# A four-batch cross-covariance attention kernel with a mixture of adapters: loads, gating and output in pieces of 10 token columns, and the passes of neighbouring batches interleaved

## The chip, the cores and the metric

The kernel runs on one core of one Trainium2 chip. The metric is device time in microseconds (us) of that core. Every kernel was run several times; a run counts as fast or slow by its state, and every ratio and every profile below is of fast runs alone. A profile has its span, from the first to the last instruction (309.3 us before). The span after is 1.8 us shorter than the device time of the same execution (296.5), so spans are compared with spans and device times with device times.

## The reference, cut to what matters

```python
# q, k, v: (B, N, C) = (4, 6400, 256) float32; tau = 1
qn = q / (norm(q, axis=1) + 1e-6)          # norms over the 6400 tokens, per channel
kn = k / (norm(k, axis=1) + 1e-6)
s  = kn.transpose(0, 2, 1) @ qn / tau      # (B, 256, 256)
a  = softmax(s, axis=-1)
x  = v @ a                                 # (B, 6400, 256), then seen as (25600, 256)
# mixture of adapters: 8 experts of rank 16, the best two of each token
logits = x @ w_gate                        # (25600, 8)
w      = softmax over the two largest logits
out    = x + sum over the two experts e of w_e * (x @ A[e]) @ B[e]
```

Within a batch everything waits for `a`, and `a` needs all of q and k of the batch. The softmax is a serial step between two passes over the tokens. Batches do not depend on each other.

## The kernel before

The 6,400 tokens of a batch lie on 128 partitions, so a batch is 50 *token columns* of 128 tokens. The loads convert float32 to bf16. For each batch there is a Gram pass over q and k (products k·q, k·k and q·q, all summed in one accumulator `acc`), a softmax chain on the 256 x 256 result, a pass that transposes v and computes the logits of all 50 columns, the gating of all 50 columns at once, and a pass that computes y and the adapters' part, two columns (a *chunk*) at a time.

```python
CPC = 2            # columns of a chunk
LPC = 16           # columns of a load: pieces of 16, 16, 16 and 2
qk_pool: bufs=4, v_pool: bufs=4, vt_pool: bufs=1, y_pool: bufs=2, gwork: bufs=1
psum_acc: bufs=1   # one accumulator for all batches

def emit_loads(b):                      # all q,k pieces, then all v pieces
    for (ps, plen) in load_pieces:
        nc.gpsimd.dma_start(qt[:, :plen, :], q_v[b, :, ps:ps + plen, :])
        nc.gpsimd.dma_start(kt[:, :plen, :], k_v[b, :, ps:ps + plen, :])
    for (ps, plen) in load_pieces:
        nc.gpsimd.dma_start(vt[:, :plen, :], v_v[b, :, ps:ps + plen, :])

def emit_G_init(b, st):                 # clears acc by a matmul with zeros
    for ic in range(CC):
        nc.tensor.matmul(acc[:, ic, :], zeros_bf[:1, :P], zeros_bf[:1, :],
                         start=True, stop=False, skip_group_check=True)
# ... emit_G_piece: 6 matmuls per column into acc (256, 128 and 128 columns, twice)
# ... emit_chain_part1..4: norms (nq_bc), s_sb, a_exp, a_bf; emit_naw: aT, waA
# ... emit_transpose_logits_group: vT_batch and logB, four columns at a time

def emit_ycopy(b, st, ch):
    y_stage, off, gi = get_y_stage(b, st, ch)     # a buffer of 16 columns, of 2
    nc.scalar.copy(y_stage[:, off * CPC:(off + 1) * CPC, :], y_ps)
    # after the last chunk of a group (8 chunks): one DMA out of up to 2 MB

for b in range(B):
    # softmax chain of b, with the last 4 chunks of batch b-1 between its parts
    # transposes and logits of all 50 columns, then the gating
    gpos = {2: 0, 7: 1, 13: 2, 17: 3}   # Gram pieces of b+1 after these chunks
    for c2 in range(main_end):
        emit_passC_chunk_tail(b, st, c2)
        if c2 + npro < main_end:
            emit_zyf(b, st, c2 + npro)
        if b + 1 < B and c2 in gpos:
            emit_G_piece(b + 1, states[b + 1], gpos[c2])
```

So the kernel before already puts Gram work of the next batch between the chunks of this batch, but in four lumps, and its transposes run alone.

Of the kernel before, what the change touches and what calls it, by code (L numbers as in the profile page):

```python
# [10 lines left out]
FP32 = mybir.dt.float32  # L11
# [7 lines left out]
def kernel(  # L19
# [20 lines left out]
    assert ER == P and C % P == 0 and N % P == 0  # L40

    if not isinstance(tau, float):
        tau = float(tau)
    inv_tau = 1.0 / tau

    CPC = 2
    LPC = 16
    NCH = NC // CPC
    KD = min(4, max(0, NCH - 2))

# [5 lines left out]
    def pieces(step, total):  # L56
        res = []
        s = 0
        while s < total:
            res.append((s, min(step, total - s)))  # L60
            s += step
        return res

    load_pieces = pieces(LPC, NC)

    def y_groups_of(b):
        last = (b + 1 == B)
        tail_start = NCH - (min(2, KD) if last else KD)
        groups = []
        s = 0  # L70
        while s < tail_start:
            e = min(s + 8, tail_start)
            groups.append((s, e - s))
            s = e
        if tail_start < NCH:
            groups.append((tail_start, NCH - tail_start))
        return groups

    const = ctx.enter_context(tc.tile_pool(name="const", bufs=1))
    qk_pool = ctx.enter_context(tc.tile_pool(name="qk", bufs=4))  # L80
    v_pool = ctx.enter_context(tc.tile_pool(name="vp", bufs=4))
    vt_pool = ctx.enter_context(tc.tile_pool(name="vtb", bufs=1))
    y_pool = ctx.enter_context(tc.tile_pool(name="yp", bufs=2))
    bat = ctx.enter_context(tc.tile_pool(name="bat", bufs=2))
    gwork = ctx.enter_context(tc.tile_pool(name="gwork", bufs=1))
    work = ctx.enter_context(tc.tile_pool(name="work", bufs=3))
    psum_acc = ctx.enter_context(tc.tile_pool(name="psacc", bufs=1, space=bass.MemoryType.PSUM))
    psum_logB = ctx.enter_context(tc.tile_pool(name="pslog", bufs=1, space=bass.MemoryType.PSUM))
# [3 lines left out]
    ident = const.tile([P, P], BF16)  # L92
    make_identity(nc, ident)

    ones_bf = const.tile([P, P], BF16)
    nc.vector.memset(ones_bf, 1.0)

    zeros_bf = const.tile([P, 512], BF16)
    nc.vector.memset(zeros_bf, 0.0)

    neg_inv_tau = const.tile([P, 1], FP32)
    nc.vector.memset(neg_inv_tau, -inv_tau)

    wg_sb = const.tile([P, CC, E], BF16)
    nc.gpsimd.dma_start(wg_sb, moe_w_gate.rearrange("(cc p) e -> p cc e", p=P))

    A_sb = const.tile([P, CC, E, R], BF16)
    moe_A_v = moe_A.rearrange("e (cc p) r -> p cc e r", p=P)
    for cc in range(CC):
        nc.gpsimd.dma_start(A_sb[:, cc, :, :], moe_A_v[:, cc, :, :])  # L110
    A_sb = A_sb.rearrange("p cc e r -> p cc (e r)")

    ball_sb = const.tile([P, C], BF16)
    nc.gpsimd.dma_start(ball_sb, moe_B.rearrange("e r d -> (e r) d"))

    def emit_loads(b):
        st = {}
        q_tiles, k_tiles, v_tiles = {}, {}, {}
        for (ps, plen) in load_pieces:
            qt = qk_pool.tile([P, LPC, C], BF16, tag="q_piece", name="qt")  # L120
            nc.gpsimd.dma_start(qt[:, :plen, :], q_v[b, :, ps:ps + plen, :])
            kt = qk_pool.tile([P, LPC, C], BF16, tag="k_piece", name="kt")
            nc.gpsimd.dma_start(kt[:, :plen, :], k_v[b, :, ps:ps + plen, :])
            q_tiles[ps] = qt
            k_tiles[ps] = kt
        for (ps, plen) in load_pieces:
            vt = v_pool.tile([P, LPC, C], BF16, tag="v_piece", name="vt")
            nc.gpsimd.dma_start(vt[:, :plen, :], v_v[b, :, ps:ps + plen, :])
            v_tiles[ps] = vt
        st["q_tiles"] = q_tiles  # L130
        st["k_tiles"] = k_tiles
        st["v_tiles"] = v_tiles
        return st

    def emit_G_init(b, st):
        acc = psum_acc.tile([P, CC, 512], FP32, tag="acc", name="acc")
        st["acc"] = acc
        for ic in range(CC):
            nc.tensor.matmul(  # L139
                acc[:, ic, :], zeros_bf[:1, :P], zeros_bf[:1, :],  # L140
                start=True, stop=False, skip_group_check=True)

    def emit_G_piece(b, st, pi):
        acc = st["acc"]
        ps, plen = load_pieces[pi]
        qt, kt = st["q_tiles"][ps], st["k_tiles"][ps]
        for lc in range(plen):
            c = ps + lc
            last = (c == NC - 1)
            for ic in range(CC):  # L150
                nc.tensor.matmul(  # L151
                    acc[:, ic, 0:256],
                    kt[:, lc, ic * P:(ic + 1) * P],
                    qt[:, lc, :],
                    start=False, stop=False, skip_group_check=True)
            for ic in range(CC):
                nc.tensor.matmul(  # L157
                    acc[:, ic, 256:384],
                    kt[:, lc, ic * P:(ic + 1) * P],
                    kt[:, lc, ic * P:(ic + 1) * P],  # L160
                    start=False, stop=False, skip_group_check=True)
            for ic in range(CC):
                nc.tensor.matmul(  # L163
                    acc[:, ic, 384:512],
                    qt[:, lc, ic * P:(ic + 1) * P],
                    qt[:, lc, ic * P:(ic + 1) * P],
                    start=False, stop=last, skip_group_check=True)

    def emit_G(b, st):
        emit_G_init(b, st)  # L170
        for pi in range(len(load_pieces)):
            emit_G_piece(b, st, pi)

    def emit_chain_part1(b, st):
        acc = st["acc"]
        nk2 = bat.tile([P, CC], FP32, name="nk2")
        kscr = bat.tile([P, CC, P], BF16, name="kscr")
        qqI = bat.tile([P, CC, P], BF16, name="qqI")
        for ic in range(CC):
            nc.vector.scalar_tensor_tensor(  # L180
                out=qqI[:, ic, :], in0=acc[:, ic, 384:512], scalar=1.0,
                in1=ident, op0=OP.mult, op1=OP.mult)
# [5 lines left out]
        st["nk2"] = nk2  # L188
        st["qqI"] = qqI

    def emit_chain_part2(b, st):
        nq2_bc = psum_A.tile([P, 256], FP32, tag="psA", name="nq2_bc")
        nc.tensor.matmul(nq2_bc, ones_bf,
                         st["qqI"].rearrange("p c d -> p (c d)"),
                         start=True, stop=True)
        lnk = bat.tile([P, CC], FP32, name="lnk")
        nc.scalar.activation(lnk, st["nk2"], ACT.Ln)
        rk = bat.tile([P, CC], FP32, name="rk")
        nc.scalar.activation(rk, lnk, ACT.Exp, scale=-0.5)
        lnq = bat.tile([P, 256], FP32, name="lnq")  # L200
        nc.scalar.activation(lnq, nq2_bc, ACT.Ln)
        rq_bc = bat.tile([P, 256], FP32, name="rq_bc")
        nc.scalar.activation(rq_bc, lnq, ACT.Exp, scale=-0.5)
        st["rk"] = rk
        st["rq_bc"] = rq_bc

    def emit_chain_part3(b, st):
        acc = st["acc"]
        rk, rq_bc = st["rk"], st["rq_bc"]
        s_sb = bat.tile([P, CC, 256], FP32, name="s_sb")  # L210
        for ic in range(CC):
            nc.vector.scalar_tensor_tensor(
                out=s_sb[:, ic, :], in0=acc[:, ic, 0:256],
                scalar=rk[:, ic:ic + 1], in1=rq_bc,
                op0=OP.mult, op1=OP.mult)
        a_exp = bat.tile([P, CC, 256], BF16, name="a_exp")
        sumexp = bat.tile([P, CC], FP32, name="sumexp")
        for ic in range(CC):
            nc.scalar.activation(a_exp[:, ic, :], s_sb[:, ic, :], ACT.Exp,
                                 bias=neg_inv_tau[:, 0:1], scale=inv_tau,  # L220
                                 accum_out=sumexp[:, ic:ic + 1])
        st["a_exp"] = a_exp
        st["sumexp"] = sumexp

    def emit_chain_part4(b, st):
        recip = bat.tile([P, CC], FP32, name="recip")
        nc.vector.reciprocal(recip, st["sumexp"])
        a_bf = bat.tile([P, CC, 256], BF16, name="a_bf")
        for ic in range(CC):
            nc.vector.tensor_scalar(out=a_bf[:, ic, :],  # L230
                                    in0=st["a_exp"][:, ic, :],
                                    scalar1=recip[:, ic:ic + 1], scalar2=None,
                                    op0=OP.mult)
        st["recip"] = recip
        st["a_bf"] = a_bf

    def emit_naw(b, st):
        a_exp, recip = st["a_exp"], st["recip"]
        aT_ps = psum_A.tile([P, CC, 256], BF16, tag="psA", name="aT_ps")
        n_tr = CC * CC  # L240
# [339 lines left out]
```

## Time and profile before

The median of the runs beside the changed kernel is 311.87 us (310.38 to 312.39, four runs).

The first lines of the page of the kernel before: busy time, then 40 slices of 7.7 us with the busy tenths of TensorE (PE), its granted clock in tenths and the share of the 16 DMA engines in use, then the two main DMA queues (packets, MB, share of the 16 engines' span).

```profile
span 309.3 us, 7431 instructions
PE 256.8 (83%) x3264; PEld 220.9 (71%) x3264; DVE 118.2 (38%) x377; ACT 103.9 (34%) x198; POOL 29.2 (9%) x58
...
PE   1079595999999966999999966999999978979981
...
PEclk9999997699999998999999995799999999999997
DMA  7999999999999999999999999999850055202467
...
q0 software_dynamic: 9408, 39.46, 63.2%
q1 hardware_dynamic: 2304, 26.22, 20.3%
```

The row of TensorE has a dip at 31 to 54 us (the first softmax chain), then two that are two slices wide (66, at 108 to 124 and 178 to 193 us) and a shallow one near 250 us: these are the boundaries between batches. The row of the DMA is full (nines) until about 217 us, has an eight until 224 us, and is thin afterwards. TensorE and the DMA therefore both matter, at different times.

The waits of TensorE and of ScalarE in the kernel before; columns: engine, line, what was waited for, then us in total, times, the longest.

```profile
PE acc L151 <- DMA kt<-in_k_dram: 18.4, 2, 14.8
PE y_ps L392 <- ACT y_stage L440: 14.6, 11, 2.9
PE acc L139 <- DVE s_sb L212: 3.3, 1, 3.3
...
ACT y_stage L440 <- PE y_ps L430: 116.7, 60, 8.4
ACT y_stage L440 <- DMA out_dram<-y_stage: 6.4, 2, 3.3
```

The copy of y waits twice, 3.3 us at most, until an output DMA has emptied a buffer. First ScalarE, then TensorE around 190 us; columns: start, us, engine, line, operation, and in brackets the idle time before it and its releaser.

```profile
189.72 1.07 ACT L440 COPY y_stage<-y_ps 128x512 f32<-128x512 f32 x2 [3.26 <-DMA out_dram<-y_stage]
190.68 0.52 ACT L219 ACTIVATE a_exp<-s_sb,neg_inv_tau 128x256 bf16<-128x256 f32 x1
```

The windows view by batch; columns: window, its length, busy time of TensorE, weight loads, VectorE, ScalarE and GpSimd with instruction counts, granted clock, DMA share (1 reads as all 16 engines in use; it can be slightly above), GB/s.

```profile
51.00:121.00 70.00, 63.11 (x805) 55.35 (x805) 29.17 (x86) 24.39 (x47) 7.39 (x14) 0.94 1.03 246
121.00:190.00 69.00, 62.95 (x816) 54.13 (x814) 29.47 (x88) 25.24 (x49) 6.34 (x12) 0.95 1.03 262
190.00:260.00 70.00, 65.10 (x834) 56.33 (x834) 30.71 (x94) 27.14 (x53) 2.11 (x4) 0.95 0.67 193
260.00:309.00 49.00, 38.44 (x511) 31.84 (x509) 26.67 (x100) 22.61 (x43) 0.00 (x0) 0.97 0.38 157
```

Busy time of TensorE overstates its work, because matmuls overlap (by the page, a key-query matmul of 256 columns lasts 277 ns in the mean, and the next one can start after 109). I therefore took the start times of successive matmuls from the trace and split the time from the first norm matmul (the start of the first softmax chain) to the last matmul into four parts:

- *issue*: what the matmuls need when nothing is in the way, with the usual intervals of the trace (109 ns for 256 columns, 55.5 for 128, 25 for 8). For the zero matmuls of 512 columns, 216 ns is an estimate: 109 plus twice the 53.5 that the step from 128 to 256 columns adds (in the trace of the kernel before, the next matmul follows them after 400 ns or more, five of the eight times at half clock).
- *long gaps*: the excess over the usual interval of the full clock, for the single intervals where it is 1 us or more, whatever the clock was.
- *half clock*: all other excess in stretches in which the granted clock was half.
- *small stalls*: the rest.

| us | first norm matmul | issue | long gaps | half clock | small stalls | last matmul starts | span |
|---|---|---|---|---|---|---|---|
| before | 46.9 | 201.2 | 17.9 | 9.7 | 27.3 | 302.9 | 309.3 |

The first norm matmuls of the four batches start at 46.9, 110.5, 179.9 and 250.7 us.

### The profile page before, as it was taken

Reading aid. Unit: us, or ns where it says so; the run is one execution under the profiler, and the core shown is the slowest. Engines: PE = TensorE matmul, PEld = TensorE weight load, DVE = VectorE, ACT = ScalarE, POOL = GpSimd, SP = SyncE. Lnnn points to the kernel's source line nnn. Section 1 sums busy time; section 2 is a strip of 40 time slices with the busy share of each in tenths; the row PEclk is TensorE's granted clock in tenths of the full one; section 3 lists DMA queues with packets and bytes.
Section 4 is the critical chain, followed back from the end, with each engine's and each line's share of the span. In section 5 each row is a group of like instructions: output and inputs, shape, how many; then the busy total and the mean of one; then the engine's idle time right before and its main releaser. Section 6 shows DMA issues by size and latency. Waiting matters only on the chain.

```text
span 309.3 us, 7431 instructions
## 1 busy us (share of the span) xinstructions
PE 256.8 (83%) x3264; PEld 220.9 (71%) x3264; DVE 118.2 (38%) x377; ACT 103.9 (34%) x198; POOL 29.2 (9%) x58
## 2 busy tenths in 40 slices
PE   1079595999999966999999966999999978979981
PEld 0069493997898854897888854997898856867770
DVE  0000004475312344475312344466412246794540
ACT  1000005432322272642322272542313266744451
POOL 8210120201110110110010110020000000000000
PEclk9999997699999998999999995799999999999997
DMA  7999999999999999999999999999850055202467
GB/s 48 214 212 220 212 213 217 215 212 219 214 307 251 215 309 298 281 256 212 217 318 246 215 316 301 269 257 214 190 245 2 32 242 219 90 2 104 172 271 305
DMA packets 11744, 66.14 MB, mean 214 GB/s; under 512 B 3392, under 2 KB 5056, under 8 KB 5184
## 3 DMA queue, kind: packets, MB, share of 16 engines
q0 software_dynamic: 9408, 39.46, 63.2%
q1 hardware_dynamic: 2304, 26.22, 20.3%
q8 instruction: 25, 0.41, 0.5%
q14 instruction: 7, 0.06, 0.1%
HBM read 78.91 MB, written 26.21 MB: 340 GB/s over the span
## 4 chain that ended last, share of the span: by engine, by line
PE 56%; DMA 19%; ACT 11%; DVE 8%; POOL 2%; issue 2%; ACTq 0%; POOLq 0%; DVEq 0%
PE y_ps L392 14%; DMA kt<-in_k_dram 10%; DMA out_dram<-y_stage 9%; PE acc L151 9%; ACT y_stage L440 9%; PE vT_ps L303 8%; PE y_ps L430 6%; PE acc L163 4%; PE acc L157 4%; PE logB L317 3%; PE zg L415 2%; PE zg L380 2%; DVE gzT_sb L424 1%; PE acc L139 1%; DVE gz_sb L405 1%
## 5 line engine op out<-in xcount | busy, mean ns | idle before, releaser
L440 ACT COPY y_stage<-y_ps 128x512 f32<-128x512 f32 x100 | 56.1, 587 | 123.3 <-PE y_ps L430 116.7
L151 PE MATMUL acc<-qt,kt 128*128 128x256 bf16 x400 | 80.5, 277 | 18.5 <-DMA kt<-in_k_dram 18.4
L392 PE MATMUL y_ps<-a_bf,vT_batch 128*128 128x256 bf16 x400 | 61.9, 275 | 17.3 <-ACT y_stage L440 14.6
L392 PEld LDWEIGHTS <-vT_batch 128*128 128x128 bf16 x400 | 38.5, 98 | 28.8 <-issue 23.4
L157 PE MATMUL acc<-kt 128*128 128x128 bf16 x400 | 56.8, 222 | 0.0
L163 PE MATMUL acc<-qt 128*128 128x128 bf16 x400 | 56.6, 222 | 0.0
L405 DVE TENSOR_TENSOR gz_sb<-zg,gate 128x256 bf16<-128x256 f32 x100 | 41.7, 422 | 35.2 <-PE zg L380 35.0
L424 DVE COPY gzT_sb<-zg 128x256 bf16<-128x256 bf16 x100 | 27.7, 285 | 58.4 <-PE zg L415 57.9
L151 PEld LDWEIGHTS <-kt 128*128 128x128 bf16 x400 | 31.9, 99 | 19.7 <-DMA kt<-in_k_dram 19.7
L380 PE MATMUL zg<-waA_sb,vT_batch 128*128 128x128 bf16 x400 | 43.1, 220 | 1.0 <-ACT vT_batch L312 1.0
L157 PEld LDWEIGHTS <-kt 128*128 128x128 bf16 x400 | 39.5, 99 | 4.9
L430 PE MATMUL y_ps<-ball_sb,gzT_sb 128*128 128x256 bf16 x200 | 38.2, 282 | 2.2 <-DVE gzT_sb L424 1.8
L303 PE MATMUL vT_ps<-ident,vt 128*128 128x128 bf16 x400 | 35.4, 236 | 0.0
L312 ACT COPY vT_batch<-vT_ps 128x512 bf16<-128x512 bf16 (+1 forms) x52 | 28.1, 572 | 17.2 <-DVE vT_batch L309 16.8
L163 PEld LDWEIGHTS <-qt 128*128 128x128 bf16 x400 | 31.8, 99 | 0.2
L380 PEld LDWEIGHTS <-vT_batch 128*128 128x128 bf16 x400 | 29.8, 98 | 3.0 <-issue 1.3
L415 PE MATMUL zg<-ident,gz_sb 128*128 128x128 bf16 x200 | 29.2, 223 | 1.7 <-DVE gz_sb L405 1.7
L303 PEld LDWEIGHTS <-vt 128*128 128x128 bf16 x400 | 27.1, 106 | 0.5
L309 DVE COPY vT_batch<-vT_ps 128x512 bf16<-128x512 bf16 (+1 forms) x52 | 20.9, 410 | 13.7 <-PE vT_ps L303 12.3
L430 PEld LDWEIGHTS <-gzT_sb 128*128 128x128 bf16 x200 | 15.7, 99 | 9.9 <-DVE gzT_sb L424 7.5
L180 DVE SCALAR_TENSOR_TENSOR qqI<-acc,ident 128x128 bf16<-128x128 f32 x8 | 2.0, 286 | 47.1 <-PE acc L163 47.1
L317 PE MATMUL logB<-waA_sb,vT_batch 128*128 128x8 bf16 x400 | 19.7, 168 | 0.3 <-ACT vT_batch L312 0.2
(116 smaller groups left out, 144.3 us busy)
## 6 DMA issues: line engine op xcount, KB each, us to landing
out_dram<-y_stage SPq DMA_DIRECT2D x8, 2048.0 KB, 11.2
qt<-in_q_dram POOLq DMA_DIRECT2D x12, 1024.0 KB, 31.8
kt<-in_k_dram POOLq DMA_DIRECT2D x12, 1024.0 KB, 28.9
vt<-in_v_dram POOLq DMA_DIRECT2D x12, 1024.0 KB, 31.3
out_dram<-y_stage SPq DMA_DIRECT2D x3, 1280.0 KB, 12.5
out_dram<-y_stage SPq DMA_DIRECT2D x3, 1024.0 KB, 12.4
out_dram<-y_stage SPq DMA_DIRECT2D x1, 1792.0 KB, 5.7
qt<-in_q_dram POOLq DMA_DIRECT2D x4, 128.0 KB, 30.4
```

The source lines that it names most:

```text
L151: nc.tensor.matmul(acc[:, ic, 0:256], kt[:, lc, ic * P:(ic + 1) * P], qt[:, lc, :], start=False, stop=False, skip_group_check=True)
L157: nc.tensor.matmul(acc[:, ic, 256:384], kt[:, lc, ic * P:(ic + 1) * P], kt[:, lc, ic * P:(ic + 1) * P], start=False, stop=False, skip_grou ...
L163: nc.tensor.matmul(acc[:, ic, 384:512], qt[:, lc, ic * P:(ic + 1) * P], qt[:, lc, ic * P:(ic + 1) * P], start=False, stop=last, skip_group ...
L303: nc.tensor.matmul(vT_ps[:, ic, sc * P:(sc + 1) * P], vt[:, voff + sc, ic * P:(ic + 1) * P], ident, is_transpose=True, start=(i_tr == 0), ...
L317: nc.tensor.matmul(logB[:, cs + sc, :], vT_batch[:, ic, cs + sc, :], awg_sb[:, ic, :], start=False, stop=False, skip_group_check=True)
L380: nc.tensor.matmul(z_ps[:, sc, :], vT_batch[:, ic, cs + sc, :], aA_sb[:, ic, :], start=(sc == 0 and ic == 0), stop=(sc == CPC - 1 and ic = ...
L392: nc.tensor.matmul(y_ps[:, sc, :], vT_batch[:, ic, cs + sc, :], a_bf[:, ic, :], start=(sc == 0 and ic == 0), stop=False, skip_group_check= ...
L405: nc.vector.tensor_tensor(out=gz_sb.rearrange("p c (e r) -> p c e r", e=E), in0=z_ps.rearrange("p c (e r) -> p c e r", e=E), in1=gate[:, c ...
L415: nc.tensor.matmul(gzT_ps[:, sc, :], gz_sb[:, sc, :], ident, is_transpose=True, start=(sc == 0), stop=(sc == CPC - 1))
L424: nc.vector.tensor_copy(gzT_sb, gzT_ps)
L430: nc.tensor.matmul(y_ps[:, sc, :], gzT_sb[:, sc, :], ball_sb, start=False, stop=(sc == CPC - 1), skip_group_check=True)
L440: nc.scalar.copy(y_stage[:, off * CPC:(off + 1) * CPC, :], y_ps)
```

## The change

The intent is to make everything that waits smaller, and to put other work beside it: loads, transposes, logits, gating and output all run in pieces of 10 columns. Each of the first four pieces of v of one batch is processed next to a Gram piece of the following batch, so the queues hold a mix of both for most of the time. The constants are loaded after the first q,k pieces instead of before them, four output buffers replace two, and the clearing of `acc` and of the logits by zero matmuls is gone (the first real matmul has `start=True`). The core of the diff, with cuts:

```diff
-    CPC = 2
-    LPC = 16
+    PC = 10
+    NP = NC // PC                       # 5 pieces
+    QK_BUFS = 6
+    V_BUFS = 8
...
-    vt_pool = ctx.enter_context(tc.tile_pool(name="vtb", bufs=1))
-    y_pool = ctx.enter_context(tc.tile_pool(name="yp", bufs=2))
+    vt_pool = ctx.enter_context(tc.tile_pool(name="vtp", bufs=4))
+    y_pool = ctx.enter_context(tc.tile_pool(name="yp", bufs=4))
...
+    order = [("qk", 0, i) for i in range(NP)]      # order of the loads
+    order.insert(2, ("const", 0, 0))
+    for b in range(B):
+        nxt = [("qk", b + 1, i) for i in range(NP)] if b + 1 < B else []
+        for i in range(NP):
+            order.append(("v", b, i))
+            order += nxt[:2] if i == 0 else nxt[:1]
+            nxt = nxt[2:] if i == 0 else nxt[1:]
...
-        for ic in range(CC):            # in emit_G_init
-            nc.tensor.matmul(
-                acc[:, ic, :], zeros_bf[:1, :P], zeros_bf[:1, :],
-                start=True, stop=False, skip_group_check=True)
...
+    def emit_gate(b, i):                # logits and gating of one piece
+        log = psum_log.tile([P, n, E], FP32, tag="log", name="log")
+        # ... 20 logit matmuls, 11 VectorE operations, 1 of ScalarE
...
-            nc.sync.dma_start(
-                out_v[b, :, gs * CPC:(gs + glen) * CPC, :],
-                stage[:, :glen * CPC, :])
+            nc.sync.dma_start(out_v[b, :, i * PC:(i + 1) * PC, :], y_sb)
...
+    for b in range(B):
+        more = b + 1 < B
+        g = iter(range(NP))
+        if more:
+            emit_G(b + 1, next(g))
+        for i in range(NP):
+            if more and i < NP - 1:
+                emit_G(b + 1, next(g))
+                if i == NP - 2:
+                    emit_chain(b + 1)
+            if i + 1 < NP:
+                emit_T(b, i + 1)
+                emit_gate(b, i + 1)
+            elif more:
+                emit_T(b + 1, 0)
+                emit_gate(b + 1, 0)
+            emit_Y(b, i)
```

## The prediction

> What bounds the kernel now. It has a front, three equal batches and a tail. The chain of waits shows the front: loads land until 38 us, the Gram matmuls of the last 18 columns end at 46, and the softmax chain lets TensorE go at 50.4. The chain then repeats every 69.5 us (first transposes of a batch at 51, 121, 190, 260). The last batch takes from 260 to 303.8, and its output lands at 309.3. From the starts of successive matmuls I read issue intervals of 109 ns (256 columns), 55 ns (128) and 25 ns (8). With them a token column costs 0.44 us (Gram), 0.16 (transposes and logits) and 0.49 (z, y, gates, delta). After 50.4 us this is about 202 us of TensorE work in 253 us; 51 us are lost: about 20 at the three batch boundaries (softmax chain, and y copies waiting for output buffers; the list of waits has DMA out 6.4 us), 9 in z/y beside Gram work, 13 in transposes, 7 in the last batch's z/y, 2 before the gate is ready. So TensorE's order and latency bound it. The queues table gives DMA 63.2% + 20.3% of the span, 258 us, so DMA stands close behind. Loads run at 213 GB/s of bf16, 426 GB/s of source[...]. The bytes stay.
>
> What changes. Matmul and copy counts stay, but for 12 zero-writing matmuls removed (about 3 us). Gating runs per 10 columns: 12 small VectorE operations 20 times, near 0.2 us each by the traced 128x80 forms; VectorE gains some 30 us but stays under TensorE.
>
> Front: queries and keys start before the constants, and only 10 columns of Gram work remain after the last landing (4.4 us, not 8): Gram done near 41 us, 5 us earlier.
>
> Middle: I walked one piece through the changed order of every engine with traced durations: 11.0 us of TensorE work takes about 12.3 us. DMA per piece, three loads of 3.08 us and an output of 3.1, is also 12.3. The two limits meet. Waits on output buffers vanish (four buffers).
>
> Boundary: the next batch's first Gram matmuls stand in TensorE's queue right after the norm matmul and wait for the single accumulator. I expect about 5.5 us idle at each of three boundaries, like today's 5 to 7, and half clock for about 10 us after the first chain, as today (windows view: granted clock 0.75 in 40 to 60 us).
>
> Tail: without Gram filler a piece takes about 8.5 us, near today's pace; the last output lands 5 us after its copy.
>
> Sum: 45 to the first freed accumulator, 202 work, 25 piece stalls, 16 boundaries, 7 first chain and clock, 5 thinner tail, 5 landing: 305. By differences from before I get 298. I predict 302 us, 80% range 288 to 315. Faster by over 2%: 0.60; within 2%: 0.31; slower: 0.09.
>
> Right if: Gram of batch 0 ends near 41 us; no y copy waits for DMA out; batches repeat every 63 to 67 us; DMA share stays above 0.9 until about 230 us; accumulator matmuls wait 2.5 to 3.5 us for s_sb of VectorE, three times.
>
> Wrong if: the interleaved gating operations delay the gate multiply so that a piece takes 13.5 us (320), or the boundary idle trips the half clock each time (5 us apiece), or 10-column loads run slower than 207 GB/s. If Gram work fills the boundaries better than I walked, 285.

## More of the kernel before

```profile
185.04 0.60 PE L392 MATMUL y_ps<-a_bf,vT_batch 128*128 128x256 bf16 x4 [2.74 <-ACT y_stage L440]
...
190.36 1.86 PE L392 MATMUL y_ps<-a_bf,vT_batch 128*128 128x256 bf16 x8 [2.29 <-ACT y_stage L440]
```

The y copy stands still for 3.26 us (and for 3.10 us at the boundary before, with the same exponential behind it). TensorE waits for that copy, and the exponential of the softmax chain (the second line of ScalarE) stands in ScalarE's queue behind it. An output transfer thus delays the chain that the whole next batch needs.

Of the 17.9 us of long gaps, 5.7 end in a y matmul that waits for the output buffers just shown.

## The result, and the profile after

| | median us | lowest to highest | runs |
|---|---|---|---|
| before | 311.87 | 310.38 to 312.39 | 4 |
| after | 296.52 | 295.82 to 296.88 | 4 |

The ratio is 0.9522, with a 95% interval of 0.9486 to 0.9557: faster by over 2%. A ratio is the mean time of one kernel's fast runs over that of the other's fast runs of the same rounds, so it is not quite the ratio of the medians.

The page of the kernel after, the same lines (the slices are now 7.4 us long).

```profile
span 294.7 us, 7480 instructions
PE 253.5 (86%) x3252; PEld 220.2 (75%) x3252; DVE 131.2 (45%) x538; ACT 104.5 (35%) x220; POOL 34.6 (12%) x69
...
PE   0596767999999399999999599999999599999991
...
PEclk9997997999999899999999779999999889999998
DMA  6999999999999999999999999999999204444444
...
q0 software_dynamic: 9968, 39.46, 66.5%
q1 hardware_dynamic: 2880, 26.22, 21.6%
```

The boundaries are now one slice wide (3, 5, 5); before, the first two were two slices wide. The DMA is full until about 228 us, no earlier than before.

The waits of TensorE and ScalarE in the kernel after.

```profile
PE acc L143 <- DMA kt<-in_k_dram: 23.0, 5, 10.4
PE aT_ps L203 <- ACT a_exp L192: 2.8, 1, 2.8
PE acc L143 <- DVE s_sb L189: 2.5, 1, 2.5
...
ACT y_sb L336 <- PE y_ps L331: 60.2, 59, 2.8
```

The line in which the y copy waited for a DMA out is gone. The key loads now appear five times.

TensorE's timeline of the kernel after, at the first softmax chain and at the three boundaries (four separate places).

```profile
46.05 0.56 PE L143 MATMUL acc<-qt,kt 128*128 128x256 bf16 x2 [3.67 <-DMA kt<-in_k_dram]
...
101.44 0.61 PE L143 MATMUL acc<-qt,kt 128*128 128x256 bf16 x2 [4.59 <-DMA kt<-in_k_dram]
...
166.74 0.59 PE L143 MATMUL acc<-qt,kt 128*128 128x256 bf16 x2 [2.55 <-DVE s_sb L189]
...
233.45 0.23 PE L203 MATMUL aT_ps<-ident,a_exp 128*128 128x128 bf16 x1 [2.80 <-ACT a_exp L192]
```

One long wait stands at each boundary. Only the one at 166.74 us is put down to the softmax chain holding the accumulator; two are put down to the key piece, and the last to the exponential. A wait with two causes is put down to the one that ended last, so VectorE has to be looked at too. Here is `s_sb`, the last step of the chain that reads the accumulator, at the first boundary.

```profile
98.47 0.88 DVE L189 SCALAR_TENSOR_TENSOR s_sb<-acc,rk,rq_bc 128x256 f32<-128x256 f32 x2 [2.07 <-ACT rk L184]
```

It ended at 99.35 us. TensorE had stood still since 96.85 us, so 2.5 of the 4.59 us belong to the accumulator and only the last 2.1 to the key piece. In the first chain `s_sb` ended at 45.62 us: 3.2 of the 3.67 us are the accumulator's.

The windows by batch in the kernel after, from one chain to the next.

```profile
46.00:102.00 56.00, 50.28 (x669) 44.41 (x670) 25.34 (x104) 19.90 (x44) 8.24 (x16) 0.96 1.05 249
102.00:167.00 65.00, 61.24 (x814) 53.58 (x812) 32.19 (x132) 25.55 (x54) 8.66 (x17) 0.97 1.04 262
167.00:233.00 66.00, 62.45 (x813) 54.58 (x811) 32.51 (x134) 25.50 (x54) 4.23 (x8) 0.96 1.00 255
233.00:294.70 61.70, 52.48 (x660) 43.59 (x660) 39.24 (x159) 29.29 (x62) 0.00 (x0) 0.95 0.37 150
```

With TensorE at 61 to 62 us of 65 to 66 in the two middle windows and the DMA share at 1.00 to 1.04, both are nearly full there. The last window is long because nearly all that the last batch does with v is still to come then, and there is no Gram work left to put beside it.

The same split of TensorE's time, for both kernels (all numbers us):

| | first norm matmul | issue | long gaps | half clock | small stalls | last matmul starts | span |
|---|---|---|---|---|---|---|---|
| before | 46.9 | 201.2 | 17.9 | 9.7 | 27.3 | 302.9 | 309.3 |
| after | 42.1 | 199.4 | 14.3 | 7.0 | 25.5 | 288.2 | 294.7 |
| difference | -4.8 | -1.8 | -3.6 | -2.7 | -1.8 | -14.7 | -14.6 |

This split says where the time went. It does not say which part of the change did it, because one part can move time between the columns. The experiments ask that.

### The profile page after: what moved, and what is told of

Same layout as the page of the kernel before. It is cut to its first block, busy times and chain, and to the rows that moved or that the text cites. A ratio compares the mean times of both kernels' runs of the same rounds, so it can differ in the third digit from the quotient of the medians.

```text
span 294.7 us, 7480 instructions
## 1 busy us (share of the span) xinstructions
PE 253.5 (86%) x3252; PEld 220.2 (75%) x3252; DVE 131.2 (45%) x538; ACT 104.5 (35%) x220; POOL 34.6 (12%) x69
## 3 DMA queue, kind: packets, MB, share of 16 engines
q0 software_dynamic: 9968, 39.46, 66.5%
HBM read 78.91 MB, written 26.21 MB: 357 GB/s over the span
## 4 chain that ended last, share of the span: by engine, by line
PE 52%; DMA 33%; ACT 7%; issue 3%; DVE 3%; POOL 1%; POOLq 0%
DMA qt<-in_q_dram 17%; DMA kt<-in_k_dram 16%; PE y_ps L312 14%; PE acc L143 8%; PE vT_ps L247 7%; PE y_ps L331 6%; ACT y_sb L336 5%; PE zg L305 4%; PE acc L152 4%; PE acc L147 4%; PE log L265 3%; PE zg L326 3%; POOL qt L117 1%; DVE gzT_sb L329 1%; PE aT_ps L203 0%
## 5 line engine op out<-in xcount | busy, mean ns | idle before, releaser
L143 PE MATMUL acc<-qt,kt 128*128 128x256 bf16 x400 | 84.9, 282 | 25.5 <-DMA kt<-in_k_dram 23.0
L336 ACT COPY y_sb<-y_ps 128x512 f32<-128x512 f32 x100 | 55.2, 587 | 60.2 <-PE y_ps L331 60.2
L312 PE MATMUL y_ps<-a_bf,vT 128*128 128x256 bf16 x400 | 61.6, 275 | 2.2 <-ACT y_sb L336 0.8
L147 PE MATMUL acc<-kt 128*128 128x128 bf16 x400 | 60.5, 224 | 0.0
L252 ACT COPY vT<-vT_ps 128x512 bf16<-128x512 bf16 (+1 forms) x60 | 28.7, 518 | 70.7 <-DVE vT L251 70.7
L143 PEld LDWEIGHTS <-kt 128*128 128x128 bf16 x400 | 33.0, 100 | 27.7 <-DMA kt<-in_k_dram 26.3
L251 DVE COPY vT<-vT_ps 128x512 bf16<-128x512 bf16 (+1 forms) x60 | 22.2, 378 | 58.5 <-PE vT_ps L247 57.3
L312 PEld LDWEIGHTS <-vT 128*128 128x128 bf16 x400 | 37.5, 98 | 12.2 <-issue 7.0
L321 DVE TENSOR_TENSOR gz_sb<-zg,gate 128x256 bf16<-128x256 f32 x100 | 41.6, 416 | 9.2 <-PE zg L305 9.1
L305 PE MATMUL zg<-waA_sb,vT 128*128 128x128 bf16 x400 | 45.7, 219 | 0.0
L331 PE MATMUL y_ps<-ball,gzT_sb 128*128 128x256 bf16 x200 | 38.6, 274 | 2.4 <-DVE gzT_sb L329 2.4
L152 PEld LDWEIGHTS <-qt 128*128 128x128 bf16 x400 | 31.7, 101 | 0.1
L305 PEld LDWEIGHTS <-vT 128*128 128x128 bf16 x400 | 29.8, 97 | 1.4
L265 PE MATMUL log<-waA_sb,vT 128*128 128x8 bf16 x400 | 23.4, 168 | 0.0
L265 PEld LDWEIGHTS <-vT 128*128 128x128 bf16 x400 | 18.5, 97 | 3.9 <-DVE vT L251 2.6
## 6 DMA issues: line engine op xcount, KB each, us to landing
vt<-in_v_dram POOLq DMA_DIRECT2D x20, 640.0 KB, 31.7
wg_raw<-in_moe_w_gate_dram POOLq DMA_DIRECT2D x1, 4.0 KB, 13.3
```

The costliest lines, as they stand in the source:

```text
L143: nc.tensor.matmul(acc[:, ic, 0:256], kt[:, lc, ic * P:(ic + 1) * P], qt[:, lc, :], start=first, stop=False, skip_group_check=True)
L147: nc.tensor.matmul(acc[:, ic, 256:384], kt[:, lc, ic * P:(ic + 1) * P], kt[:, lc, ic * P:(ic + 1) * P], start=False, stop=False, skip_grou ...
L152: nc.tensor.matmul(acc[:, ic, 384:512], qt[:, lc, ic * P:(ic + 1) * P], qt[:, lc, ic * P:(ic + 1) * P], start=False, stop=last, skip_group ...
L265: nc.tensor.matmul(log[:, sc, :], vT[:, ic, sc, :], s["awg"][:, ic, :], start=(sc == 0 and ic == 0), stop=(sc == n - 1 and ic == CC - 1), ...
L305: nc.tensor.matmul(z_ps[:, sc, :], vT[:, ic, c + sc, :], s["aA"][:, ic, :], start=(sc == 0 and ic == 0), stop=(sc == 1 and ic == CC - 1), ...
L312: nc.tensor.matmul(y_ps[:, sc, :], vT[:, ic, c + sc, :], s["a_bf"][:, ic, :], start=(sc == 0 and ic == 0), stop=False, skip_group_check=True)
```

## The experiments

Twelve kernels were run in three rounds of four, each three times against the kernel before on the same chip, all correct. Letters in the quoted expectations name the theories within that text, and differ from round to round. In the first round I still held that stall filling by Gram work was worth 6 to 12 us (a_noilv) and the front about 4.4 us (b_front). Its results changed that; the theories from the second round on were:

- *Mine*: most of the gain comes from things that the kernel before could have had too, namely the earlier front and the output buffers, while interleaving by itself is worth only 2 to 5 us.
- *The rival*: interleaving is what pays; without it the pieces would give back most of the gain (304 us or more).

| kernel | starts from | median us | ratio to before | 95% interval |
|---|---|---|---|---|
| b_front | before | 305.88 | 0.9847 | 0.9772 to 0.9923 |
| b_y3 | before | 304.46 | 0.9815 | 0.9733 to 0.9897 |
| b_front_y3 | before | 303.12 | 0.9711 | 0.9664 to 0.9759 |
| b_all | before | 309.73 | 0.9943 | 0.9909 to 0.9976 |
| b_pin | before | 302.45 | 0.9711 | 0.9668 to 0.9755 |
| a_noilv | after | 308.61 | 0.9952 | 0.9894 to 1.0009 |
| a_noilv_v | after | 306.48 | 0.9835 | 0.9812 to 0.9859 |
| a_noilv_v_pin | after | 305.95 | 0.9815 | 0.9773 to 0.9858 |
| a_gate2 | after | 313.42 | 1.0073 | 1.0030 to 1.0116 |
| a_split | after | 293.05 | 0.9453 | 0.9399 to 0.9507 |
| a_shift | after | 295.22 | 0.9457 | 0.9420 to 0.9495 |
| a_split_pin | after | 290.67 | 0.9339 | 0.9302 to 0.9377 |

The kernel before had medians of 310.57, 311.38 and 311.93 us in the three rounds. Below, a gain in us from a ratio is one minus the ratio, times the median of before of that round. The splits of TensorE's time are from one profile each:

| us | first norm matmul | issue | long gaps | half clock | small stalls | last matmul starts | span |
|---|---|---|---|---|---|---|---|
| b_front | 41.5 | 201.2 | 16.6 | 11.6 | 26.9 | 297.8 | 304.2 |
| b_y3 | 46.7 | 201.2 | 12.2 | 8.1 | 27.5 | 295.7 | 302.1 |
| b_front_y3 | 41.4 | 201.2 | 16.3 | 9.0 | 26.6 | 294.5 | 300.9 |
| b_all | 43.2 | 199.4 | 26.0 | 6.1 | 27.5 | 302.2 | 308.6 |
| b_pin | 41.3 | 201.2 | 16.7 | 8.0 | 27.7 | 295.0 | 301.4 |
| a_noilv | 42.7 | 199.4 | 21.9 | 12.0 | 24.6 | 300.6 | 307.1 |
| a_noilv_v | 42.2 | 199.4 | 24.5 | 6.5 | 25.3 | 297.9 | 304.4 |
| a_noilv_v_pin | 42.0 | 200.7 | 14.0 | 9.3 | 31.7 | 297.7 | 304.2 |
| a_gate2 | 41.9 | 199.4 | 22.7 | 11.3 | 29.5 | 304.8 | 311.3 |
| a_split | 42.7 | 199.4 | 13.7 | 3.7 | 25.2 | 284.6 | 291.1 |
| a_shift | 42.2 | 199.4 | 14.5 | 6.6 | 24.3 | 287.0 | 293.5 |
| a_split_pin | 41.6 | 200.3 | 10.3 | 2.9 | 29.0 | 284.0 | 289.1 |

### b_front: the front alone, in the kernel before

The last q,k loads, of every batch, are of 10 and 8 columns instead of 16 and 2, and the constants are loaded after the first q,k piece.

```diff
+    qk_pieces = [(0, 16), (16, 16), (32, 10), (42, 8)]
...
-        for (ps, plen) in load_pieces:
+        for (ps, plen) in qk_pieces:
+            if b == 0 and ps == 16:
+                load_consts()          # the DMAs of the constants, moved here
```

> The kernel before with the front alone changed: constants are loaded after the first query and key piece, and the query and key pieces are 16, 16, 10 and 8 columns, not 16, 16, 16 and 2, so 8 columns of Gram work are left after the last landing, not 18. Theory A (the front gave about 4.4 us of the gain, stall filling the rest): the first accumulator is freed at 46 us, not 50.4, and the time falls to 306 to 308.5 us. Rival theory B (the gain is on the DMA side: output buffers and a load stream that never stops): the front only shifts into the later waits, 310.5 us or more.

It measured 305.88 us, just below my range of 306 to 308.5 us and well below the rival's 310.5. By the ratio this is 4.8 us less than before, 2.4 to 7.1 by its interval. The first norm matmul came at 41.5 instead of 46.9 us. That the gain is nearly as large as this shift is partly luck, for other waits changed as well:

```profile
ACT y_stage L444 <- DMA out_dram<-y_stage: 1.0, 1, 1.0
```

The y copy now waited only 1.0 us for an output DMA, where it was 6.4 us before, and the two long gaps of 5.7 us in y matmuls are gone. A new long gap of 4.3 us before a Gram matmul (at 62.5 us, for a key piece) and 1.9 us more of half clock take most of that back.

### b_y3: a third output buffer, in the kernel before

```diff
-    y_pool = ctx.enter_context(tc.tile_pool(name="yp", bufs=2))
+    y_pool = ctx.enter_context(tc.tile_pool(name="yp", bufs=3))
```

> The kernel before with three output buffers in place of two, so that no y copy waits for an output DMA (6.4 us of ACT waits in two places before). Theory A: the boundaries lose as much to the softmax chain as to the buffers (19.6 us before, 18.6 after the change), so at most 4 us come back: 308 to 311.5 us. Rival B: the two boundaries shrink by the whole 6.4 us and by the half clock that follows them: 303 us or less.

It measured 304.46 us: 5.7 us less by the ratio (3.2 to 8.3 by its interval). My limit of 4 us was too low, and the rival's 303 us or less was not reached either. The waits of ScalarE now have one line for the y copy; the one for the output DMA is gone.

```profile
ACT y_stage L440 <- PE y_ps L430: 116.9, 62, 8.4
```

In the split the long gaps fall from 17.9 to 12.2 us, exactly the 5.7 us of the output-buffer waits, and the half clock falls by 1.6. One number in the kernel before, 2 to 3 buffers, is worth more than a third of the gain of the whole rewrite.

### b_front_y3: both

> The kernel before with both earlier edits, the front (constants later, 8 Gram columns after the last landing) and three output buffers. Alone they gave ratios 0.985 and 0.982. Theory C (two separate losses, found after the first four runs): they add, ratio 0.963 to 0.972, about 300 to 302 us. Rival D (both only move the same waiting on output and loads about): no better than the better one, ratio 0.978 or more.

It measured 303.12 us, a ratio of 0.9711 where the product of the two single ratios is 0.9665. The ratio lies in theory C's range, the median 1.1 us above it. The two effects nearly add, but they are not two separate losses: in b_front most of the waiting for output DMAs was gone already, with two buffers. The wait of 4.0 us for a key piece in the first batch (at 62.5 us) is the one that b_front has too (4.3 us): with the front earlier, TensorE arrives at that piece before its load has landed. Front and buffers together explain about 9.0 us of the gain of 14.9. The kernel after is another 2% faster (0.9522 over 0.9711 is 0.981, about 6 us); that remainder is due to all the rest of the change together: the pieces, the interleaving, the order of the loads and the zero matmuls.

### b_all: also without the zero matmuls

```diff
-        for ic in range(CC):
-            nc.tensor.matmul(
-                acc[:, ic, :], zeros_bf[:1, :P], zeros_bf[:1, :],
-                start=True, stop=False, skip_group_check=True)
...
-                    start=False, stop=False, skip_group_check=True)
+                    start=(c == 0), stop=False, skip_group_check=True)
```

The zero matmul of the logits is removed in the same way.

> The same with the zero-writing matmuls taken out as well (the first Gram and logit matmul starts the accumulation, as in the changed kernel); the order of batch passes stays that of the kernel before: no piecewise interleaving at all. Theory C: the three edits hold most of the gain; ratio 0.955 to 0.967, so 298 to 301.5 us, and piecewise interleaving is left with 2 to 5 us of the 15. Rival A (interleaving fills the stalls and is worth 8 us, as undoing it cost 12): ratio stays at 0.968 or more.

The removal of work made the kernel slower: 309.73 against 303.12 us. The matmuls take 1.8 us less of issue time (199.4 against 201.2), but the long gaps grow from 16.3 to 26.0 us. TensorE's timeline of this kernel shows the reason.

```profile
62.39 0.61 PE L151 MATMUL acc<-qt,kt 128*128 128x256 bf16 x2 [13.04 <-DMA kt<-in_k_dram]
62.79 0.21 PE L256 MATMUL waA_ps<-wg_sb,aT_sb 128*128 128x8 bf16 x1
...
63.32 0.95 PE L300 MATMUL vT_ps<-ident,vt 128*128 128x128 bf16 x7
```

The first Gram matmuls of the next batch now stand in TensorE's queue ahead of the last matmuls of the softmax chain (waA) and of the transposes of v, and wait 13.04 us for their key piece. In b_front_y3 the zero matmul stood there, which waits for no load, and the first Gram matmul came only after the transposes and the first z and y matmuls. In b_all no matmul starts between 49.35 us, where this wait begins, and 62.39 us, while in b_front_y3 the waA matmuls ran from 48.18 us on. The value of the zero matmuls alone therefore cannot be read from this run. What it shows is that the *order* put in by removing them costs more than they do. My range of 298 to 301.5 us fell; the rival's ratio of 0.968 or more holds, but for a reason that it did not name.

### b_pin: Gram held behind the last transposes

b_front_y3, but the zeros that clear `acc` are computed from the previous batch's last transposed columns, so that Gram cannot go ahead of them.

```diff
+        zr = zeros_bf
+        if b > 0:
+            zr = bat.tile([P, 512], BF16, name="zr")
+            nc.vector.tensor_scalar(
+                out=zr[:1, :],
+                in0=states[b - 1]["vT_batch"][:1, 0, NC - 4:NC, :].rearrange("p c t -> p (c t)"),
+                scalar1=0.0, scalar2=None, op0=OP.mult)
         for ic in range(CC):
             nc.tensor.matmul(
-                acc[:, ic, :], zeros_bf[:1, :P], zeros_bf[:1, :],
+                acc[:, ic, :], zeros_bf[:1, :P], zr[:1, :],
                 start=True, stop=False, skip_group_check=True)
```

> The kernel before with front and three output buffers, and the first Gram matmul of the next batch held back: the zero row that starts its accumulator is made from the last transposed v columns, so it can't stand in TensorE's queue ahead of the transposes. In the run of the two edits TensorE waited 4.0 us there for a key piece and then ran 3.4 us at half clock. Theory E (head-of-line waits for a key piece, not missing filler, are what is left): ratio 0.952 to 0.964, so 297 to 300.5 us, within 4 us of the changed kernel and without any piecewise interleaving. Rival A (interleaving itself is worth 8 us): no change, 0.968 or more.

The ratio is the same, 0.9711, with a median of 302.45 us: theory E's 0.952 to 0.964 fell, and the rival's 0.968 or more was right. The long gap in front of a Gram matmul is still there (4.1 us instead of 4.0). The edit did its work: the last logits now come before that gap, and the gating starts at 57.65 us instead of 63.38. But the gates are only ready at 63.0 us, and the key piece landed at 62.5, so no gated work was ready for TensorE in the meantime. That wait is for a load that has not landed; the place of the Gram matmuls among the transposes does not cause it.

### a_noilv: pieces without interleaving

The kernel after, with all five Gram pieces of the next batch in one lump, before the chunks of the last v piece.

```diff
-        if more:
-            emit_G(b + 1, next(g))
         for i in range(NP):
-            if more and i < NP - 1:
-                emit_G(b + 1, next(g))
-                if i == NP - 2:
-                    emit_chain(b + 1)
+            if more and i == NP - 1:
+                for j in range(NP):
+                    emit_G(b + 1, next(g))
+                emit_chain(b + 1)
```

> The changed kernel with the interleaving undone: the five Gram pieces of the next batch are emitted in one block at the end of a batch; pieces of 10, buffers, order of the loads and gating stay. Theory A (Gram work between the pieces fills stalls): a piece without Gram work takes 8.0 us as in the tail, 1.5 us of it stall instead of 1.1, and the boundary has no filler; the time rises by 6 to 12 us to 302 to 309 us. Rival B (piece size and buffers are what counts): within 2 us of 296.5.

It measured 308.61 us, no faster than before. But it does not decide the question: the loads are still in the interleaved order, so v now comes too late. TensorE's waits show it.

```profile
PE vT_ps L247 <- DMA vt<-in_v_dram: 9.7, 2, 5.1
```

### a_noilv_v: with the loads in the matching order

a_noilv, but with all v of a batch loaded first, then all q,k of the next.

```diff
         for i in range(NP):
             order.append(("v", b, i))
-            order += nxt[:2] if i == 0 else nxt[:1]
-            nxt = nxt[2:] if i == 0 else nxt[1:]
+        order += nxt
```

> The changed kernel with Gram work in one block per batch as in the earlier run that took 308.6 us, but with the load order made to fit: all v pieces of a batch first, then the query and key pieces of the next, so that transposes do not wait for v (9.7 us there). Theory C (undoing the interleaving cost 12 us mostly because loads came in another order than they were used): 298 to 302 us. Rival A (Gram filler itself is worth it): 305 to 309 us.

It measured 306.48 us, in the rival's range of 305 to 309 us and not in my 298 to 302. The waits for v are gone, but it is confounded in the way of b_all: one wait for a key piece at the head of TensorE's queue is 15.9 us long.

```profile
PE acc L142 <- DMA kt<-in_k_dram: 30.9, 4, 15.9
```

### a_noilv_v_pin: with Gram held back as well

a_noilv_v, with zeros made as in b_pin. (The diff is cut: with them, the first Gram matmul of the later batches no longer starts the sum.)

```diff
+        if i == 0 and b > 0:            # zr: zeros made from vT of b-1's last piece
+            zr = bat.tile([P, 512], BF16, name="zr")
+            nc.vector.tensor_scalar(
+                out=zr[:1, :],
+                in0=st[b - 1]["vT", NP - 1][:1, 0, 0:4, :].rearrange("p c t -> p (c t)"),
+                scalar1=0.0, scalar2=None, op0=OP.mult)
+            for ic in range(CC):
+                nc.tensor.matmul(acc[:, ic, :], W["ones"][:1, :], zr[:1, :],
+                                 start=True, stop=False, skip_group_check=True)
```

> The changed kernel with Gram work in one block, loads in fitting order, and that block held back by a zero row made from the last v piece of the batch, so that it can't stand ahead of the transposes and wait for a key piece (15.9 us in the run without this). Theory E: 20 pieces of 8.0 us, three Gram blocks of 22 us, four chains: 298 to 302 us, so the interleaving itself is worth 2 to 5 us. Rival A (filler is worth 8 to 12 us): 304 us or more.

It measured 305.95 us. Its waits of TensorE:

```profile
PE acc L151 <- DMA kt<-in_k_dram: 15.7, 4, 10.3
PE aT_ps L211 <- ACT a_exp L200: 11.9, 4, 3.5
```

Neither confound is left: the longest key wait is now the one of the front, 10.3 us, which the kernel after has too (10.4). The long gaps are those of the kernel after (14.0 against 14.3). What is lost lies in the small stalls, 31.7 against 25.5 us, in the half clock (9.3 against 7.0) and in the zero matmuls put back (1.3 us of issue): 9.8 us in all, against 9.4 us between the medians. So interleaving is worth about 8 us once the zeros are taken off, and my 2 to 5 us fell; the rival's 304 us or more was right. Most of these 8 us are not in the long waits of the boundaries but in short stalls: the waits for the copy of the transposed gates, for example, are 4.5 us in 19 places here against 2.4 us in 9 in the kernel after. That the Gram matmuls, which depend on none of this, fill such stalls is how I read it. The kernel before had some of this already, in four lumps, so the run tells what interleaving is worth within the piecewise kernel, not what the finer mixing added to the old one. For the same reason it does not show that cutting into pieces loses time by itself: the run is about 3 us slower than b_front_y3 (303.12), but that kernel still has its four lumps.

### a_gate2: all gating done twice

Every VectorE and ScalarE operation of `emit_gate` is issued a second time into results that nothing reads.

```diff
         nc.vector.tensor_tensor(out=gate, in0=eq2, in1=eq1, op=OP.add)
+        gate_d = gwork.tile([P, n, E], FP32, name="gate_d")
+        m1 = gwork.tile([P, n], FP32, name="m1_d")
+        nc.vector.tensor_reduce(out=m1, in_=log, axis=AX.X, op=OP.max)
+        # ... the other ten VectorE operations and the exponential again ...
```

> The changed kernel with every gating operation done twice (the second result unused): 12 more small VectorE operations and one ScalarE one per piece, about 2.6 us of VectorE per piece. If gating per piece is off the critical path as the prediction has it (hidden under Gram work), the 15 pieces beside Gram work don't move and only the 5 pieces of the tail, where VectorE is 75% busy, grow by up to 2 us each: 297 to 307 us. If it paces each piece, all 20 grow: 315 us or more.

It measured 313.42 us, 16.9 us more than the kernel after. Both expected ranges missed: it is more than 297 to 307 us, and less than 315. The norm matmuls tell where: the fourth comes at 231.0 against 229.6 us in the kernel after. Up to there, the doubled gating of 14 of the 20 pieces cost 1.4 us. From there to the last matmul, with the other six, it takes 73.8 us against 58.6, that is 15.2 us more: 10.3 of long gaps, 4.3 of half clock and 0.6 of small stalls. The waits of TensorE and one window in that tail (260 to 280 us), first the doubled gating:

```profile
PE y_ps L356 <- DVE gzT_sb L354: 11.3, 13, 2.0
...
260.00:280.00 20.00, 15.70 (x188) 12.43 (x185) 13.29 (x68) 8.76 (x20) 0.00 (x0) 0.91 0.29 122
```

and the same window of the kernel after:

```profile
260.00:280.00 20.00, 19.41 (x263) 16.12 (x263) 14.99 (x62) 11.24 (x23) 0.00 (x0) 1.00 0.48 198
```

VectorE is busy for only 13.3 of 20 us, and still each piece of the tail grew by 2.5 us, about the length of what was added to it (2.3 us of VectorE). The added operations stand in VectorE's queue among the multiply by the gates and the copy of the transposed gates, for which TensorE waits. Beside Gram work the same operations are nearly free.

### a_split: the softmax chain cut in three, with chunks between

```diff
                 if i == NP - 2:
-                    emit_chain(b + 1)
+                    emit_chain_a(b + 1)     # to the norms rk, rq_bc
+                    emit_Y(b, i, 4)
+                    emit_chain_b(b + 1)     # s_sb, a_exp, recip
+                    emit_Y(b, i, 8)
+                    emit_chain_c(b + 1)     # transposes of a, a_bf, waA
```

> The changed kernel with the softmax chain of the next batch emitted in three parts, and two chunks of the z and y work emitted between each two parts, so that TensorE has work while the chain runs and the first Gram matmuls of the batch after are no longer at the head of its queue. Theory A (boundaries lose 6 us each of TensorE time to the chain's latency): 3 to 5 us come back at each of three, 282 to 288 us. Rival B (behind the boundary stands the load stream, which kept TensorE waiting for a key piece until 101 us): only the later two boundaries shrink and the loads take the time back: 291 to 296 us.

It measured 293.05 us (ratio 0.9453), in rival B's range of 291 to 296 us; theory A's 282 to 288 fell. In its split the half clock falls from 7.0 to 3.7 us; the long gaps are about the same. The waits for s_sb and a_exp at the boundaries are gone; y matmuls wait for y copies in their place (5.0 us in all, 1.5 at most). Key pieces that have not landed still leave TensorE idle: one wait of 3.57 us, at 167.22 us, is put down to one.

### a_shift: every Gram piece one piece later

a_split, with Gram piece i of the next batch next to v piece i, the chain in the last one, and the loads in that order.

```diff
-            order += nxt[:2] if i == 0 else nxt[:1]
-            nxt = nxt[2:] if i == 0 else nxt[1:]
+            order += nxt[:1]
+            nxt = nxt[1:]
...
-            if more and i < NP - 1:
+            if more:
                 emit_G(b + 1, next(g))
```

> An attempt at a faster one: the kernel with the softmax chain in three parts, and the Gram work of the next batch one piece later (piece i of it beside piece i of v, the chain in the last piece), so that the first Gram matmul of the batch after needs its key piece one piece later; it waited 3.6 us for it at the second boundary. Expected: the load waits at the boundaries go and with them most of the stall, 287 to 291 us. If the loads are what bounds the middle whatever the order, 292 to 295 us.

It measured 295.22 us, not the 287 to 291 that I hoped for, but next to the 292 to 295 of a middle bound by the loads; the ratio of 0.9457 is that of a_split, whose interval overlaps almost wholly. The long gaps before Gram matmuls stayed (5.8 us in total against 5.3). Moving the Gram work later, with the loads moved likewise, does not bring the keys in time. The DMA row shows nines until about 226 us in both kernels, so the loads leave no room in either order.

### a_split_pin: the best version

a_split, with Gram held behind a piece of the previous batch for the last two batches (`zr` as above, from the first transposed piece), and the last output in two DMAs of 6 and 4 columns.

```diff
+        if i == 0 and b > 1:
+            # zr from st[b - 1]["vT", 0], two zero matmuls into acc
...
+        if b == B - 1 and i == NP - 1:
+            if c == 4 or c + 2 == PC:
+                lo = 0 if c == 4 else 6
+                nc.sync.dma_start(out_v[b, :, i * PC + lo:i * PC + c + 2, :],
+                                  y_sb[:, lo:c + 2, :])
```

> The fastest so far (softmax chain in three parts) with the first Gram matmul of batches 2 and 3 held back until the first v piece of the batch is transposed, and the last output in two transfers of 6 and 4 columns. Expected: the 3.6 us wait for a key piece at the second boundary goes, with half clock after it, and the end comes 1 to 1.5 us earlier after the last copy: 287 to 290.5 us. If the load stream bounds the middle in any order, 291 to 293.

It measured 290.67 us (290.37 to 291.96), a ratio of 0.9339, 0.2 us above my range of 287 to 290.5. It beats both kernels. Its page has the span and the clock row, and its waits have the key loads:

```profile
span 289.1 us, 7490 instructions
...
PEclk9997997999999999999999889999999999999998
...
PE acc L152 <- DMA kt<-in_k_dram: 18.6, 4, 10.4
```

The long gaps fall to 10.3 us and the half clock to 2.9. The time from the start of the last matmul to the end of the span falls from 6.5 us in the kernel after to 5.1 us, because a smaller last DMA lands sooner (3.0 us after its issue instead of 4.5). Part of it is paid back in small stalls (29.0 against 25.2 us).

## Why the prediction was right or wrong

The verdict was right, faster by over 2%, and 296.5 us lies in the range of 288 to 315, 5.5 below the 302 predicted. Of the two ways of reckoning in the prediction, the one by differences from before (298) was closer than the sum (305).

- **What bounds it.** Right. TensorE's order and latency bound it, with the DMA close behind; the DMA share stays above 0.9 until about 228 us, for which the prediction had said 230. One thing that the traces show was not used: the last packet of the loads ended at 224.0 us before, at 229.3 after, and between 222 and 236 us in every kernel here. No order ended the loads more than 2 us sooner. The whole gain lies in what was left to do after them: 85.3 us before, 65.4 after, 56.8 in a_split_pin. A load packet took as long as an output packet of twice its bytes: in the kernel before, 625 ns for 8,192 B written and 624 ns for an output packet of 16,384 B; in the kernel after, with pieces of 10 columns, 399 ns for 5,120 B and 398 ns for 10,240 B. The loads read float32 and write bf16; the page has 78.91 MB read from HBM, and 39.46 MB in the queue of the loads.
- **Front.** Right. The last Gram matmul of batch 0 ended at 41.5 us for "near 41", and the first norm matmul is at 42.1 us, 4.8 us earlier than before; b_front has it 5.4 us earlier and gains 4.8 us, with other waits changed along with it.
- **Output buffers.** Half right. No y copy waits for a DMA out any more, as said. But the prediction put no number on it and let the boundaries cost as much as before. b_y3 shows 5.7 us for the third buffer alone: the two waits stood inside the softmax chain, by way of ScalarE's queue. (b_front lost most of them without a third buffer, so that the 5.7 us are not a share that adds to those of the front.)
- **Period.** The batches repeat after 67.4 and 66.4 us, at and just above the upper edge of "63 to 67". The first takes 53.7, because the next batch's chain now comes one piece before the end of its own; that was overlooked.
- **A piece.** 11.9 us in the steady state (two of a batch's five pieces; the others carry the boundary) for "about 12.3", and 8.0 us in the tail for "about 8.5". The mechanism was right and the size a little high.
- **Boundary.** The mechanism was right in part, the size was not. "Accumulator matmuls wait 2.5 to 3.5 us for s_sb of VectorE, three times": they did, 3.2 us in the first chain, then 2.5 and 2.55, but at two of these places the key piece landed later still (by 0.4 and 2.1 us), which the prediction did not have. At the last boundary no next batch stands behind; TensorE waits for the exponential there (2.80 us). "About 5.5 us idle at each" is the term that failed: the long gaps at the boundaries are 4.8, 2.7 and 3.0 us, in all 10.5 us where the sum had 16. Something overlooked made the chain shorter: ScalarE loads a function table (1.28 us each time) twice between the norm matmul and `s_sb` in the later chains before (at 111.8 and 113.6 us), but once after (at 96.6; the other load ran at 91.7 us, ahead of the chain). No run tells what that alone is worth.
- **Half clock.** "About 10 us after the first chain, as today" was wrong: 3.4 us there. It also came at the three boundaries, for 3.4, 6.8 and 3.4 us. The excess in all half-clock stretches after the first chain's start is 7.0 us, where 7 were predicted for the first chain alone; that the two agree is luck, for the first chain has only 1.6 of them. One of the prediction's own signs of being wrong, that "the boundary idle trips the half clock each time (5 us apiece)", did come true, but for 1.3, 2.6 and 1.5 us.
- **VectorE.** "Gains some 30 us" was too much: it went from 118.2 to 131.2 us, a gain of 13. (The gating of a piece is 11 operations of VectorE and one of ScalarE, not 12 of VectorE.)
- **The sum.** 45 + 202 + 25 + 16 + 7 + 5 + 5 = 305. Measured: 46.05 to the freed accumulator, 199.4 issue time, 25.5 of small stalls (for 25 piece stalls and 5 of the thinner tail), 10.5 for the 16 of boundaries, 7.0 for the 7 of clock, 6.5 from the last matmul to the end: 295.0 for a span of 294.7. The terms that were too large are the boundaries by 5.5 us and the stalls with the tail by 4.5. If the half clock at the boundaries (5.4 us) is counted with them, they come to 15.9 for 16, and it is the clock of the first chain that was too large, 1.6 for 7; the sum is 10 us high either way.
- **Reasons.** After the first round of experiments I believed that interleaving is worth little. a_noilv_v_pin shows about 8 us within the piecewise kernel.
- **What stays open.** About 6 of the 15 us, the step from b_front_y3 to the kernel after, are not split into pieces, finer mixing and order of loads. The worth of removing the zero matmuls could not be isolated, because their removal changed the order. The half clock's exact trigger stays open as well: in the kernel after it began at 165.6 us in a gap of 2.55 us (matmuls ran until 164.2), and at 233.9 us after a gap of 2.80 us, while in the kernel before a gap of 2.73 us (253.1 to 255.8 us) brought none. Apart from the last one of each run, the half-clock stretches of these two kernels lasted 3.4, 6.8 or 10.2 us. That the tail is paced by the gating is shown by a_gate2 for added work. Whether larger gating groups in the last batch would save time was not tried.

## What to carry to other kernels

Look first at which small wait stands *inside* the serial chain: one more output buffer gave 5.7 us, because ScalarE's copy held up the exponential behind it. When work is cut into pieces, put independent work between them on the same engine: taking it away again cost about 8 us here. Look also at when the loads end: if no order brings that forward, as here, the gain has to come from what is left to do afterwards. And check the order of TensorE's queue after every removal, since a matmul that waited for its load held up the matmuls behind it (13.0 us in b_all, for 1.8 us of work saved).
